# Shorter weight conversion, compact state, keys scaled on ScalarE and a one-instruction leaky rectifier in a retention + two-layer MLP kernel

## The chip, the cores and the metric

One core of a Trainium2 chip runs the whole program. The metric is the device time of one execution in microseconds (us). Beside the times there is one profiled execution of the kernel before, with every instruction's start and duration; all rows of this document come from it.

## The reference, cut to what matters

```python
# attention (retention): B, H, S, D = 4, 8, 768, 64
gamma = 1.0 - 2.0 ** (-5.0 - np.arange(H))
for t in range(S):
    state = gamma * state + einsum('bhd,bhe->bhde', k[:, :, t], v[:, :, t])
    y[:, :, t] = scale * einsum('bhd,bhde->bhe', q[:, :, t], state)
x = y.transpose(0, 2, 1, 3).reshape(3072, 512)
# layer 1 (moe) and layer 2 (moe2): w_in 512 x 2048, w_out 2048 x 512
h = x @ moe_w_in;  x = np.maximum(0.01 * h, h) @ moe_w_out
h = x @ moe2_w_in; x = (h - np.tanh(h)) @ moe2_w_out
```

The weights arrive as 64-bit floating point numbers; the kernel reads them as pairs of 32-bit words and makes 32-bit numbers of them with integer operations.

## The kernel before

**Attention** runs first, in 24 steps over 6 chunks of 128 positions and 4 pairs of heads; a step holds one chunk of one pair for all 4 batches. In step s TensorE transposes the next key tile (L270, `kTp`) and half a query tile (L284, `qTp`), computes the output `y` of step s (L327 inside the chunk, L320 from the carried state `U`), the scores `sc` of step s+1 (L305), and the state's increment `u` (L355). ScalarE copies the transposes out of PSUM (L272 `kT`, L285 `qT`) and the output (L344 `x1st`). VectorE masks the scores (L309, `A`, two instructions a step) and updates the state (L358, two instructions, one for each head's 64 partitions). The state of a pair is kept as 128 x 128 for each batch with two diagonal 64 x 64 blocks and zeros elsewhere, so that one 128-row matmul serves both heads. GpSimd scales the keys of step s+2 (L251) and the queries (L261, four instructions of 128x256 for a query tile). SyncE issues all loads, four steps ahead for keys and values.

**Weight conversion.** A unit is one half (w_in or w_out) of one of 16 weight slices, so 32 units for each layer. `ConvPipe.step()` works on three units at once: `s3` of unit n-2, `s1` of unit n, `s2` of unit n-1. `s1` clamps the high words on VectorE (L103) and squares the result on ScalarE (L106); `s2` is four VectorE instructions (L111, L113, L115, L117); `s3` is `split`, a ScalarE copy into a rounded high part (L126) and a GpSimd subtraction for the low part (L127). A counter sets the pace: the first 13 units are spread over the attention steps from step 6 on, and the rest come at 1.5 units for each MLP step (`RATE` 12 per 8 steps). Each engine runs its instructions strictly in the order of the program, apart from weight loads on TensorE.

**MLP.** 192 steps (2 layers x 6 blocks of 512 rows x 16 slices). A step is 12 matmuls into `h` (L436, three products of high and low parts for each of 4 contraction tiles) and, two steps later, 12 matmuls into four accumulators (L454). Between them stand `el_1` (layer 1: ScalarE copies 0.01 h out of PSUM at L482, VectorE takes the maximum with h at L483) and `el_2` (`split` of the result on ScalarE and GpSimd). Slice m of layer 1 can be used only after units 2m and 2m+1 have gone through `s3`. The units of layer 2 are converted during layer 1, one per two steps, and stored to DRAM until they are reloaded.

Of the kernel before, what the change touches and what calls it, by code (L numbers as in the profile page):

```python
# [18 lines left out]
P = 128  # L19
# [8 lines left out]
F64_MAX_HI = 3.38953138925153547590470800371487866880e38  # L28
# [19 lines left out]
def kernel(  # L48
# [34 lines left out]
    class Convert:  # L83


        def __init__(self, w_in, w_out, m, half, done):
            self.args = (w_in, w_out, m, half)
            self.done = done
            self.id = f"{w_in.tensor.name}_{m}_{half}"
# [9 lines left out]
        def s1(self):  # L99
            pairs = self.raw.rearrange("p (f t) -> p f t", t=2)  # L100
            self.lo, hi = pairs[:, :, 0], pairs[:, :, 1]
            self.y = cm.tile([P, DM], F32, tag="t0", name=f"cy_{self.id}")
            nc.vector.tensor_scalar(out=self.y, in0=hi.bitcast(F32), scalar1=F64_MAX_HI, scalar2=-F64_MAX_HI,  # L103
                                    op0=ALU.min, op1=ALU.max)
            self.sq = cm.tile([P, DM], F32, tag="t1", name=f"csq_{self.id}")
            nc.scalar.activation(out=self.sq, in_=self.y, func=AF.Square)  # L106

        def s2(self):
            y, t = self.y, cm.tile([P, DM], I32, tag="t2", name=f"ct_{self.id}")
            yi = y.bitcast(I32)  # L110
            nc.vector.scalar_tensor_tensor(out=y, in0=self.sq, scalar=F64_MIN_HI_SQ, in1=y,  # L111
                                           op0=ALU.is_ge, op1=ALU.mult)
            nc.vector.tensor_scalar(out=t, in0=yi, scalar1=3, scalar2=0x3FFFFFFF,  # L113
# [26 lines left out]
    for m in range(NM):  # L140
        for half in range(2):
            conv1.append(Convert(moe_w_in, moe_w_out, m, half,
                                 lambda f, m=m, half=half: split(slots[m][:, :, half, :], f, nc.gpsimd)))
            conv2.append(Convert(moe2_w_in, moe2_w_out, m, half,
                                 lambda f, m=m, half=half: nc.sync.dma_start(out=w2s[m, :, half], in_=f)))
# [42 lines left out]
    with tc.tile_pool(name="at", bufs=2, reuse_waits="tile") as at, \  # L188
# [51 lines left out]
        for p in range(NPAIR):  # L240
            u = at.tile([P, NB, P], F32, tag=f"U{p}", name=f"U{p}", bufs=1)
            nc.gpsimd.memset(u, 0.0)
            U.append(u)

        def a_scale_k(s, eng=nc.gpsimd):
# [5 lines left out]
            eng.tensor_tensor(out=t, in0=t, in1=fb, op=ALU.mult)  # L251
# [61 lines left out]
        def a_Y(s):  # L313
# [4 lines left out]
            def inter(first):  # L318
                for b in range(NB):
                    nc.tensor.matmul(y[:, b, :], U[p][:, b, :], d["qT"][:, b, tq], start=first and b == 0,  # L320
                                     stop=b == NB - 1 and not first)
# [25 lines left out]
        def a_U(s):  # L347
            c, p = steps[s]
            d = S[s]
            if c < NC - 1:  # L350
# [5 lines left out]
                for h in range(2):  # L356
                    r = slice(h * ND, (h + 1) * ND)
                    nc.vector.scalar_tensor_tensor(out=U[p][r, :, r], in0=U[p][r, :, r], scalar=gc[r, p:p + 1],  # L358
                                                   in1=u[r, :, :], op0=ALU.mult, op1=ALU.add)
# [116 lines left out]
    def el_1(n):  # L476
# [3 lines left out]
        u = mo.tile([P, TB], F32, tag="u", name=f"u_{n}", bufs=1)  # L480
        if layer == 0:
            nc.scalar.activation(out=u, in_=h, func=AF.Copy, scale=0.01)  # L482
            nc.vector.tensor_tensor(out=gt, in0=u, in1=h, op=ALU.max)  # L483
        else:
            nc.scalar.activation(out=u, in_=h, func=AF.Square)  # L485
# [66 lines left out]

F64_MIN_HI_SQ = 0.0


def _min_sq():
    import numpy as np
    t = float(np.uint32(0x38100000).view(np.float32))
    return t * t


F64_MIN_HI_SQ = _min_sq()


# [51 lines left out]
```

## Time and profile before

| what | value |
|---|---|
| median of 3 runs (lowest to highest) | 1221.44 us (1221.44 to 1222.99) |
| profiled execution: its time, its span | 1223.63 us, 1221.1 us |
| TensorE busy | 1176.3 us, 96% of the span |
| VectorE busy | 759.3 us, 62% |
| ScalarE busy | 518.3 us, 42% |
| GpSimd busy | 425.0 us, 35% |
| mean granted TensorE clock | 0.992 of full speed |

Busy shares are averages over stages that have different limits. The span has three stages: attention until about 140 us, a stretch to about 246 us in which layer 1 has begun while its weights are still being converted, and the rest, in which both layers run on converted weights. The page's row of VectorE in 40 slices rises from 4 to 9 tenths over the first two stages and stays at 7 or below in the third; the row of TensorE has sevens to nines in the first two and nines in the third.

### The profile page before, as it was taken

Reading aid. Unit: us, or ns where it says so; the run is one execution under the profiler, and the core shown is the slowest. Engines: PE = TensorE matmul, PEld = TensorE weight load, DVE = VectorE, ACT = ScalarE, POOL = GpSimd, SP = SyncE. Lnnn points to the kernel's source line nnn. Section 1 sums busy time; section 2 is a strip of 40 time slices with the busy share of each in tenths; the row PEclk is TensorE's granted clock in tenths of the full one; section 3 lists DMA queues with packets and bytes.
Section 4 is the critical chain, followed back from the end, with each engine's and each line's share of the span. In section 5 each row is a group of like instructions: output and inputs, shape, how many; then the busy total and the mean of one; then the engine's idle time right before and its main releaser. Section 6 shows DMA issues by size and latency. Waiting matters only on the chain.

```text
span 1221.1 us, 16090 instructions
## 1 busy us (share of the span) xinstructions
PE 1176.3 (96%) x6059; PEld 967.5 (79%) x6059; DVE 759.3 (62%) x1115; ACT 518.3 (42%) x851; POOL 425.0 (35%) x337
## 2 busy tenths in 40 slices
PE   8978887799999999999999999999999999999998
PEld 6867765578888888888888888888888888888886
DVE  4688899944444544445411477767767677676665
ACT  3343433333333333333344554544544545545543
POOL 4565345433223223223257623223222232232221
PEclk9999998999999999999999999999999999999999
DMA  9997333332142232241062110100100100200000
GB/s 239 269 261 219 117 123 106 103 109 81 69 138 86 78 125 74 78 147 61 18 216 89 54 65 1 47 23 1 69 1 1 69 1 1 70 1 1 35 1 35
DMA packets 108270, 100.22 MB, mean 82 GB/s; under 512 B 54688, under 2 KB 83488, under 8 KB 108192
## 3 DMA queue, kind: packets, MB, share of 16 engines
q1 hardware_dynamic: 105168, 93.87, 24.7%
q10 hardware_dynamic: 3024, 5.32, 1.2%
q8 instruction: 47, 0.77, 0.3%
q14 instruction: 31, 0.25, 0.1%
HBM read 72.96 MB, written 26.21 MB: 81 GB/s over the span
## 4 chain that ended last, share of the span: by engine, by line
PE 83%; DVE 12%; issue 2%; DMA 1%; SPq 1%; ACT 1%; POOL 0%; DVEq 0%; ACTq 0%; POOLq 0%
PE h L436 40%; PE acc L454 39%; DVE _in_moe_w_in_dram L111 3%; DVE _in_moe_w_in_dram L115 2%; DVE _in_moe_w_in_dram L113 2%; DVE _in_moe_w_in_dram L103 1%; DVE A L309 1%; PE sc L305 1%; PE y L327 1%; DVE _in_moe_w_in_dram L117 1%; PE y L320 1%; DVE g L483 1%; PE u L355 1%; DVE U L358 1%; PE kTp L270 0%
## 5 line engine op out<-in xcount | busy, mean ns | idle before, releaser
L436 PE MATMUL h<-xk,w 128*128 128x512 f32 x2304 | 557.8, 391 | 7.2 <-ACT w L126 5.4
L436 PEld LDWEIGHTS h<-xk,w 128*128 128x128 f32 x2304 | 434.5, 189 | 99.8 <-ACT w L126 6.2
L127 POOL TENSOR_TENSOR ghl<-g,ghl 128x512 fp32r<-128x512 f32 x191 | 254.4, 1332 | 616.2 <-ACT ghl L126 616.2
L454 PE MATMUL acc<-ghl,w 128*128 128x512 f32 x1152 | 282.3, 394 | 13.3 <-POOL ghl L127 7.6
L454 PE MATMUL acc<-w,ghl 128*128 128x512 f32 x1152 | 277.2, 389 | 0.5 <-ACT st L467 0.5
L454 PEld LDWEIGHTS acc<-ghl,w 128*128 128x128 f32 x1152 | 218.3, 190 | 62.1 <-POOL ghl L127 9.3
L454 PEld LDWEIGHTS acc<-w,ghl 128*128 128x128 f32 x1152 | 216.0, 188 | 46.6 <-ACT st L467 0.9
L126 ACT ACTIVATE ghl<-g 128x512 fp32r<-128x512 f32 x192 | 120.9, 629 | 296.2 <-DVE g L497 214.2
L483 DVE TENSOR_TENSOR g<-u,h 128x512 f32<-128x512 f32 x96 | 65.8, 686 | 250.7 <-ACT u L482 250.7
L489 DVE SCALAR_TENSOR_TENSOR w<-u,h 128x512 f32<-128x512 f32 x96 | 65.9, 687 | 139.9 <-ACT u L485 139.9
L482 ACT ACTIVATE u<-h 128x512 f32<-128x512 f32 x96 | 57.1, 594 | 142.5 <-PE h L436 140.4
L497 DVE COPY_PREDICATED g<-mk,th 128x512 f32<-128x512 uint8 x96 | 76.7, 799 | 3.3
L117 DVE SCALAR_TENSOR_TENSOR _in_moe_w_in_dram<-_in_moe_w_in_dram,_in_moe_w_in_dram 128x512 int32<-128x512 int32 x60 | 76.2, 1270 | 2.1
L487 ACT ACTIVATE s<-u,lead 128x512 f32<-128x512 f32 x96 | 69.7, 726 | 3.1
L492 DVE SCALAR_TENSOR_TENSOR w<-u,w 128x512 f32<-128x512 f32 x96 | 67.3, 701 | 3.3
L495 DVE SCALAR_TENSOR_TENSOR g<-s,w 128x512 f32<-128x512 f32 x96 | 65.6, 683 | 0.1
L496 DVE TENSOR_TENSOR th<-h,th 128x512 f32<-128x512 f32 x96 | 65.6, 683 | 0.0
L127 POOL TENSOR_TENSOR w<-_in_moe_w_in_dram,w 128x512 fp32r<-128x512 f32 x29 | 39.1, 1347 | 75.7 <-ACT w L126 75.7
L106 ACT ACTIVATE _in_moe_w_in_dram<-_in_moe_w_in_dram 128x512 f32<-128x512 f32 x60 | 37.8, 630 | 63.4 <-DVE _in_moe_w_in_dram L103 63.4
L485 ACT ACTIVATE u<-h 128x512 f32<-128x512 f32 x96 | 56.6, 590 | 14.6 <-PE h L436 14.4
L491 ACT ACTIVATE th<-h 128x512 f32<-128x512 f32 x96 | 57.5, 599 | 4.5 <-DVE w L489 4.4
L111 DVE SCALAR_TENSOR_TENSOR _in_moe_w_in_dram<-_in_moe_w_in_dram,_in_moe_w_in_dram 128x512 f32<-128x512 f32 x60 | 57.2, 953 | 0.0
(59 smaller groups left out, 758.3 us busy)
## 6 DMA issues: line engine op xcount, KB each, us to landing
_in_moe_w_in_dram<-in_moe_w_in_dram SPq DMA_DIRECT2D x29, 512.0 KB, 3.5
_in_moe_w_in_dram<-in_moe_w_out_dram SPq DMA_DIRECT2D x29, 512.0 KB, 3.7
w2s<-_in_moe_w_in_dram SPq DMA_DIRECT2D x32, 256.0 KB, 2.6
w2r<-w2s SPq DMA_DIRECT2D x16, 512.0 KB, 3.3
q<-in_q_dram SPq DMA_DIRECT2D x24, 256.0 KB, 5.0
k<-in_k_dram SPq DMA_DIRECT2D x48, 128.0 KB, 4.0
v<-in_v_dram SPq DMA_DIRECT2D x48, 128.0 KB, 4.1
x2s<-st SPq DMA_DIRECT2D x24, 256.0 KB, 2.0
```

The costliest lines, as they stand in the source:

```text
L111: nc.vector.scalar_tensor_tensor(out=y, in0=self.sq, scalar=F64_MIN_HI_SQ, in1=y, op0=ALU.is_ge, op1=ALU.mult)
L117: nc.vector.scalar_tensor_tensor(out=t, in0=yi, scalar=-0x40000000, in1=t, op0=ALU.bitwise_and, op1=ALU.bitwise_or)
L126: nc.scalar.activation(out=dst[:, 0], in_=src, func=AF.Copy)
L127: eng.tensor_tensor(out=dst[:, 1], in0=src, in1=dst[:, 0].bitcast(F32), op=ALU.subtract)
L436: nc.tensor.matmul(h, a, x[:, b, :], start=kt == 0 and i == 0, stop=kt == NK - 1 and i == 2)
L454: nc.tensor.matmul(ACC[j], a, b, start=m == 0 and i == 0, stop=m == NM - 1 and i == 2)
L483: nc.vector.tensor_tensor(out=gt, in0=u, in1=h, op=ALU.max)
L487: nc.scalar.activation(out=s, in_=u, func=AF.Square, bias=beta)
L489: nc.vector.scalar_tensor_tensor(out=w, in0=u, scalar=C3, in1=h, op0=ALU.mult, op1=ALU.mult)
L492: nc.vector.scalar_tensor_tensor(out=w, in0=u, scalar=A1, in1=w, op0=ALU.add, op1=ALU.mult)
L495: nc.vector.scalar_tensor_tensor(out=gt, in0=s, scalar=K1, in1=w, op0=ALU.add, op1=ALU.mult)
L497: nc.vector.copy_predicated(out=gt, mask=mk, data=th)
```

## The change

Four parts, all visible in the diff:

1. **Conversion.** `s1` becomes one ScalarE instruction (the absolute value of the high words, into tile `t`), and `s2` four VectorE instructions that work in place on `t`: a clamp from below and above, a shift with a mask, and two instructions that merge the low word and the sign and exponent bits from the raw words. The two helper tiles go; `t` rotates over three tags with two buffers each.
2. **Compact state.** `U` is 128 x 64 for each batch instead of 128 x 128 with zeros. One VectorE instruction updates it (the first chunk is a ScalarE copy instead), and the product with the queries becomes two 64 x 64 matmuls for each batch instead of one 128 x 128.
3. **Keys.** From step 2 on the keys are scaled by two ScalarE instructions (one for each head, with the scale in a 128 x 1 operand) instead of one GpSimd instruction.
4. **Leaky rectifier.** In layer 1 one ScalarE instruction (`Prelu`, alpha 0.01) replaces the ScalarE copy and the VectorE maximum.

```diff
         def s1(self):
             pairs = self.raw.rearrange("p (f t) -> p f t", t=2)
-            self.lo, hi = pairs[:, :, 0], pairs[:, :, 1]
-            self.y = cm.tile([P, DM], F32, tag="t0", name=f"cy_{self.id}")
-            nc.vector.tensor_scalar(out=self.y, in0=hi.bitcast(F32), scalar1=F64_MAX_HI, scalar2=-F64_MAX_HI,
-                                    op0=ALU.min, op1=ALU.max)
-            self.sq = cm.tile([P, DM], F32, tag="t1", name=f"csq_{self.id}")
-            nc.scalar.activation(out=self.sq, in_=self.y, func=AF.Square)
+            self.lo, self.hi = pairs[:, :, 0], pairs[:, :, 1]
+            self.t = cm.tile([P, DM], I32, tag=f"t{self.i % 3}", name=f"ct_{self.id}")
+            nc.scalar.activation(out=self.t.bitcast(F32), in_=self.hi.bitcast(F32), func=AF.Abs)
 
         def s2(self):
-            y, t = self.y, cm.tile([P, DM], I32, tag="t2", name=f"ct_{self.id}")
-            yi = y.bitcast(I32)
-            nc.vector.scalar_tensor_tensor(out=y, in0=self.sq, scalar=F64_MIN_HI_SQ, in1=y,
-                                           op0=ALU.is_ge, op1=ALU.mult)
-            nc.vector.tensor_scalar(out=t, in0=yi, scalar1=3, scalar2=0x3FFFFFFF,
+            t, y = self.t, self.t.bitcast(F32)
+            nc.vector.tensor_scalar(out=y, in0=y, scalar1=MIN_HI, scalar2=MAX_HI, op0=ALU.max, op1=ALU.min)
+            nc.vector.tensor_scalar(out=t, in0=t, scalar1=3, scalar2=0x3FFFFFFF,
                                     op0=ALU.logical_shift_left, op1=ALU.bitwise_and)
             nc.vector.scalar_tensor_tensor(out=t, in0=self.lo, scalar=29, in1=t,
                                            op0=ALU.logical_shift_right, op1=ALU.bitwise_or)
-            nc.vector.scalar_tensor_tensor(out=t, in0=yi, scalar=-0x40000000, in1=t,
+            nc.vector.scalar_tensor_tensor(out=t, in0=self.hi, scalar=-0x40000000, in1=t,
                                            op0=ALU.bitwise_and, op1=ALU.bitwise_or)
...
-            u = at.tile([P, NB, P], F32, tag=f"U{p}", name=f"U{p}", bufs=1)
-            nc.gpsimd.memset(u, 0.0)
-            U.append(u)
-
-        def a_scale_k(s, eng=nc.gpsimd):
+            U.append(at.tile([P, NB, ND], F32, tag=f"U{p}", name=f"U{p}", bufs=1))
+
+        def a_scale_k(s, eng=nc.scalar):
...
-            eng.tensor_tensor(out=t, in0=t, in1=fb, op=ALU.mult)
+            if eng is nc.scalar:
+                for h in range(2):
+                    eng.activation(out=t[:, :, h], in_=t[:, :, h], func=AF.Copy, scale=fk[:, 2 * p + h:2 * p + h + 1])
+            else:
+                eng.tensor_tensor(out=t, in0=t, in1=fb, op=ALU.mult)
...
                 for b in range(NB):
-                    nc.tensor.matmul(y[:, b, :], U[p][:, b, :], d["qT"][:, b, tq], start=first and b == 0,
-                                     stop=b == NB - 1 and not first)
+                    for h in range(2):
+                        r = slice(h * ND, (h + 1) * ND)
+                        nc.tensor.matmul(y[r, b, :], U[p][r, b, :], d["qT"][r, b, tq], start=first and b == 0,
+                                         stop=b == NB - 1 and not first)
...
-                for h in range(2):
-                    r = slice(h * ND, (h + 1) * ND)
-                    nc.vector.scalar_tensor_tensor(out=U[p][r, :, r], in0=U[p][r, :, r], scalar=gc[r, p:p + 1],
-                                                   in1=u[r, :, :], op0=ALU.mult, op1=ALU.add)
+                if c == 0:
+                    nc.scalar.activation(out=U[p], in_=u, func=AF.Copy)
+                else:
+                    nc.vector.scalar_tensor_tensor(out=U[p], in0=U[p], scalar=gc[:, p:p + 1], in1=u, op0=ALU.mult,
+                                                   op1=ALU.add)
...
         gt = mo.tile([P, TB], F32, tag="g", name=f"g_{n}", bufs=2)
-        u = mo.tile([P, TB], F32, tag="u", name=f"u_{n}", bufs=1)
         if layer == 0:
-            nc.scalar.activation(out=u, in_=h, func=AF.Copy, scale=0.01)
-            nc.vector.tensor_tensor(out=gt, in0=u, in1=h, op=ALU.max)
+            nc.scalar.activation(out=gt, in_=h, func=AF.Prelu, alpha=0.01)
         else:
+            u = mo.tile([P, TB], F32, tag="u", name=f"u_{n}", bufs=1)
```

How the change moves instructions on two engines. First ScalarE at the start of attention (`kT` are the copies of transposed keys, of steps 0, 1 and 2 in this order; `k` is a key tile being scaled in place). Before:

```order
L285 ACTIVATE qT_152<-qTp_0_153 128x2x2x128
L272 ACTIVATE kT_164<-kTp_159 128x512
L285 ACTIVATE qT_152<-qTp_2_166 128x2x2x128
L272 ACTIVATE kT_198<-kTp_193 128x512
L126 ACTIVATE xk_0_209<-y_200 128x512
L285 ACTIVATE qT_212<-qTp_0_213 128x2x2x128
```

With the change:

```order
L283 ACTIVATE qT_148<-qTp_0_149 128x2x2x128
L270 ACTIVATE kT_160<-kTp_155 128x512
L283 ACTIVATE qT_148<-qTp_2_162 128x2x2x128
L247 ACTIVATE k_128<-k_128,cst 128x4x64 x2
L270 ACTIVATE kT_195<-kTp_190 128x512
L122 ACTIVATE xk_0_206<-y_197 128x512
L283 ACTIVATE qT_209<-qTp_0_210 128x2x2x128
```

The scaling of the keys of step 2, which has to wait for their load, now stands ahead of the copy of the transposed keys of step 1.

Second, VectorE in the stretch in which layer 1 runs and its weights are converted (`cy`, `csq` and `ct` are the conversion's tiles, `g` is the rectifier's result). Before, one MLP step with one unit and the beginning of the next:

```order
L483 TENSOR_TENSOR g_1886<-u_1887,h_1854 128x512
L103 TENSOR_SCALAR cy_in_moe_w_in_dram_0_1894<-raw_in_moe_w_in_dram_0_1839 128x512
L111 SCALAR_TENSOR_TENSOR cy_in_moe_w_in_dram_1_1845<-csq_in_moe_w_in_dram_1_1847,cy_in_moe_w_in_dram_1_1845 128x512
L113 TENSOR_SCALAR ct_in_moe_w_in_dram_1_1898<-cy_in_moe_w_in_dram_1_1845 128x512
L115 SCALAR_TENSOR_TENSOR ct_in_moe_w_in_dram_1_1898<-raw_in_moe_w_in_dram_1_1837,ct_in_moe_w_in_dram_1_1898 128x512
L117 SCALAR_TENSOR_TENSOR ct_in_moe_w_in_dram_1_1898<-cy_in_moe_w_in_dram_1_1845,ct_in_moe_w_in_dram_1_1898 128x512
L103 TENSOR_SCALAR cy_in_moe_w_in_dram_1_1907<-raw_in_moe_w_in_dram_1_1841 128x512
```

With the change:

```order
L109 TENSOR_SCALAR ct_in_moe_w_in_dram_0_1975<-ct_in_moe_w_in_dram_0_1975 128x512
L110 TENSOR_SCALAR ct_in_moe_w_in_dram_0_1975<-ct_in_moe_w_in_dram_0_1975 128x512
L112 SCALAR_TENSOR_TENSOR ct_in_moe_w_in_dram_0_1975<-raw_in_moe_w_in_dram_0_1921,ct_in_moe_w_in_dram_0_1975 128x512
L114 SCALAR_TENSOR_TENSOR ct_in_moe_w_in_dram_0_1975<-raw_in_moe_w_in_dram_0_1921,ct_in_moe_w_in_dram_0_1975 128x512
L109 TENSOR_SCALAR ct_in_moe_w_in_dram_1_2017<-ct_in_moe_w_in_dram_1_2017 128x512
```

A unit is four VectorE instructions instead of five, and the rectifier has none left on VectorE.

## Rows read from the trace of the kernel before

**Rows 1.** The page: its head line, and GB/s moved in 40 slices

```profile
span 1221.1 us, 16090 instructions
...
GB/s 239 269 261 219 117 123 106 103 109 81 69 138 86 78 125 74 78 147 61 18 216 89 54 65 1 47 23 1 69 1 1 69 1 1 70 1 1 35 1 35
```

**Rows 2.** The chain that ended last: start us, us, what

```profile
139.91 5.49 PE h L436 x24
...
253.09 2.72 PE h L436 x12
...
696.45 2.06 PE acc L454 x9
...
703.74 1.65 PE acc L454 x6
...
1205.86 2.73 PE h L436 x12
...
1214.08 3.31 PE acc L454 x12
```

**Rows 3.** VectorE in order of time, attention: start us, us, instruction [idle before]

```profile
46.62 1.29 DVE L309 TENSOR_TENSOR A<-sc,cst 128x512 f32<-128x512 f32 x2 [2.50 <-PE sc L305]
...
65.81 1.29 DVE L309 TENSOR_TENSOR A<-sc,cst 128x512 f32<-128x512 f32 x2
...
70.46 1.29 DVE L309 TENSOR_TENSOR A<-sc,cst 128x512 f32<-128x512 f32 x2 [2.45 <-PE sc L305]
...
101.53 1.29 DVE L309 TENSOR_TENSOR A<-sc,cst 128x512 f32<-128x512 f32 x2
102.73 0.96 DVE L358 SCALAR_TENSOR_TENSOR U<-U,cst,u 64x256 f32<-64x256 f32 x2
103.73 1.07 DVE L103 TENSOR_SCALAR _in_moe_w_in_dram<-_in_moe_w_in_dram 128x512 f32<-128x512 f32 x1
...
108.63 1.29 DVE L309 TENSOR_TENSOR A<-sc,cst 128x512 f32<-128x512 f32 x2
...
136.40 1.28 DVE L309 TENSOR_TENSOR A<-sc,cst 128x512 f32<-128x512 f32 x2
```

**Rows 4.** GpSimd in order of time, the same attention step

```profile
104.47 3.59 POOL L261 TENSOR_TENSOR qp<-q,cst 128x256 f32<-128x256 f32 x4
```

**Rows 5.** VectorE groups of instructions, 46.62 to 136.40 us: xcount, busy us, mean ns, idle before

```profile
L111 DVE SCALAR_TENSOR_TENSOR _in_moe_w_in_dram<-_in_moe_w_in_dram,_in_moe_w_in_dram 128x512 f32<-128x512 f32 x7 | 7.7, 1101 | 0.0
...
L111 DVE SCALAR_TENSOR_TENSOR y_in_moe_w_in_dram<-q_in_moe_w_in_dram,y_in_moe_w_in_dram 128x512 f32<-128x512 f32 x4 | 4.4, 1100 | 0.0
```

**Rows 6.** Busy time, 150 to 243 us: PE, PEld, DVE, ACT, POOL, PE clock, DMA, GB/s

```profile
150.00:243.00 93.00, 74.92 (x292) 57.69 (x290) 89.66 (x103) 35.18 (x62) 46.69 (x33) 0.93 0.36 113
```

**Rows 7.** VectorE groups of instructions, 150 to 243 us

```profile
L483 DVE TENSOR_TENSOR g<-u,h 128x512 f32<-128x512 f32 x12 | 8.2, 679 | 0.0
```

**Rows 8.** VectorE in order of time, three neighbours with no GpSimd instruction beside them

```profile
199.60 0.43 DVE L113 TENSOR_SCALAR _in_moe_w_in_dram<-_in_moe_w_in_dram 128x512 int32<-128x512 int32 x1
200.06 0.69 DVE L115 SCALAR_TENSOR_TENSOR _in_moe_w_in_dram<-_in_moe_w_in_dram,_in_moe_w_in_dram 128x512 int32<-128x512 int32 x1
200.79 0.69 DVE L117 SCALAR_TENSOR_TENSOR _in_moe_w_in_dram<-_in_moe_w_in_dram,_in_moe_w_in_dram 128x512 int32<-128x512 int32 x1
```

**Rows 9.** ScalarE groups of instructions, whole span (L487 has a 128x1 operand)

```profile
L487 ACT ACTIVATE s<-u,lead 128x512 f32<-128x512 f32 x96 | 69.7, 726 | 3.1
...
L126 ACT ACTIVATE w<-_in_moe_w_in_dram 128x512 fp32r<-128x512 f32 x29 | 18.3, 631 | 65.7 <-DVE _in_moe_w_in_dram L117 62.9 <-POOL ghl L127 2.0 <-ACT x1st L344 0.8
```

**Rows 10.** The chain at the start of attention: TensorE's product with the state

```profile
17.86 1.09 PE y L320 x8
```

**Rows 11.** TensorE groups of instructions, 0 to 140 us: the same product

```profile
L320 PE MATMUL y<-qT,U 128*128 128x128 f32 x160 | 22.3, 283 | 0.0
```

**Rows 12.** All engines in order of time, 8 to 18 us

```profile
13.97 1.16 PE L305 MATMUL sc<-qT,kT 64*128 64x128 f32 x16
...
14.65 1.04 POOL L251 TENSOR_TENSOR k<-k,cst 128x512 f32<-128x512 f32 x1
```

More of the change, by code (lines that the diff above doesn't have):

```diff
@@ L26 @@
 TB = NB * P
-F64_MAX_HI = 3.38953138925153547590470800371487866880e38
+MAX_HI = 122879.9921875
+MIN_HI = 2.0 ** -15
 C3 = -0.019799353554844856
@@ L83, with __init__ @@
     class Convert:
-        def __init__(self, w_in, w_out, m, half, done):
-            self.args = (w_in, w_out, m, half)
+        def __init__(self, i, w_in, w_out, m, half, done):
+            self.i, self.args = i, (w_in, w_out, m, half)
             self.done = done
@@ L116, in s2 @@
                                            op0=ALU.logical_shift_right, op1=ALU.bitwise_or)
-            nc.vector.scalar_tensor_tensor(out=t, in0=yi, scalar=-0x40000000, in1=t,
+            nc.vector.scalar_tensor_tensor(out=t, in0=self.hi, scalar=-0x40000000, in1=t,
                                            op0=ALU.bitwise_and, op1=ALU.bitwise_or)
-            self.t = t
         def s3(self):
@@ L141 @@
         for half in range(2):
-            conv1.append(Convert(moe_w_in, moe_w_out, m, half,
+            conv1.append(Convert(len(conv1), moe_w_in, moe_w_out, m, half,
                                  lambda f, m=m, half=half: split(slots[m][:, :, half, :], f, nc.gpsimd)))
-            conv2.append(Convert(moe2_w_in, moe2_w_out, m, half,
+            conv2.append(Convert(len(conv2), moe2_w_in, moe2_w_out, m, half,
                                  lambda f, m=m, half=half: nc.sync.dma_start(out=w2s[m, :, half], in_=f)))
@@ L550 @@
             pipe2.step()
[L553 to L562, printed above, removed]
 def _consts():
```

## The prediction

> **What bounds the kernel now.** I read the chain that ended last first, then VectorE in order of time in each of the first two stages, then the groups of instructions for the prices.
>
> From about 250 us on the chain is nothing but TensorE: groups of 12 matmuls, 2.72 us each [rows 2]. The 192 MLP steps hold 384 such groups, so the MLP cannot take less than 384 x 2.72 = 1044.5 us. It begins at 139.9 [rows 2]; 139.9 + 1044.5 = 1184.4, and the span is 1221.1 [rows 1]. The missing 36.7 us are found in four places [rows 2]. Between the layers TensorE waits from 696.45 + 2.06 = 698.5 to 703.7, 5.2 us. Before the last group it waits from 1208.6 to 1214.1, 5.5 us. The last group takes 3.31 instead of 2.72, and 3.7 us follow it. These 15.0 us lie outside the change. The other 21.7 are lost between 140 and 250 us, while layer 1 runs on weights that are still being converted. So two sums can shrink: the attention stage (139.9) and this loss (21.7).
>
> In the lossy stretch VectorE is the limit: from 150 to 243 us it is busy 89.7 of 93 us, while TensorE has gaps and a granted clock of 0.93 [rows 6]. The stretch holds 12 rectifiers [rows 7], thus 12 MLP steps of 7.75 us where TensorE needs 2 x 2.72 = 5.44. At 1.5 units a step it holds 18 units. Undisturbed, a one-source instruction takes 0.46 us from start to start and a two-source one 0.73 [rows 8]. A unit of two and three is 3.11 us, 18 units 56.0, the rectifiers 8.2 [rows 7]; 28.8 of the 93 us remain. GpSimd ran 33 instructions there [rows 6], so each costs VectorE 28.8 / 33 = 0.87 us.
>
> In attention, the 15 steps from 46.62 to 136.40 take 89.8 us [rows 3]. Eleven of them carry a full conversion, 7 and 4 by the names of their buffers [rows 5], four don't. A step without one takes 4.65 us, and VectorE then sits idle 2.45 us for the scores [rows 3], so TensorE sets that pace. Taking 4.7 for the four, the eleven take (89.8 - 18.8) / 11 = 6.45 each: there VectorE is the limit. The reader can see it from 101.53 to 108.63 [rows 3]: masks, state update, five conversion instructions and the next masks without idle time, while GpSimd scales queries beside them [rows 4]. Its floor is 1.20 + 1.00 + 3.11 = 5.31 [rows 3, 8]; the other 1.14 us of an average step are again waits beside GpSimd.
>
> **The change part by part.**
>
> *Conversion.* Five VectorE instructions become two one-source and two two-source ones, 2 x 0.46 + 2 x 0.73 = 2.38 instead of 3.11 [rows 8]. Two of them work in place, for which there is no row; I take the same price. ScalarE trades one instruction for another of the same size and no longer waits for VectorE before it. The raw buffer is held one instruction longer, 0.7 us, hidden behind loads that are issued three units ahead.
>
> *State.* Two VectorE instructions of 1.00 together [rows 3] become one with as many elements for each partition as one of the two, 0.50. The four cleared tiles at the start were not on the chain. For the first chunk a ScalarE copy replaces the update, off the path. On TensorE, 8 instructions in 1.09 us [rows 10] become 16 on a quarter of the array. The scores also run 16 instructions, on halves of the rows, in 1.16 us [rows 12], so they overlap in pairs. The diagonal quarters have no row. The cost per step lies between nothing, if they overlap as the scores do, and another 1.09, if not. I take nothing, as the scores are the nearest row, and keep the other end as a rival.
>
> *Keys.* GpSimd loses one instruction per step. ScalarE gains two on half a tile each: between 0.32 (half of 0.63) and 0.63, plus 0.1 for the 128x1 operand (0.726 against 0.631) [rows 9], say 0.45 each. ScalarE, busy 42% of the span, has room for that. What counts is the place. At the start, the scaling of step 2 waits for its load ahead of the copy of the transposed keys of step 1, for which the scores at 13.97 wait [rows 12]. GpSimd began this scaling at 14.65 with no wait for the load [rows 12], so the keys landed at 14.65 at the latest. 14.65 + 0.9 + 0.6 for the copy = 16.15, 2.2 us behind 13.97. If they landed 0.7 earlier it is 1.5. I take 1.9. Later steps then run 1.9 behind the loads, and I count no second wait.
>
> *Rectifier.* One ScalarE instruction replaces one, and 0.68 us per step leave VectorE [rows 7]. Against this speaks the Trainium skill, "ScalarE: Activation LUTs", Rules for kernel authors: relu, max and their like belong on VectorE, which is faster for each element. No run here shows Prelu. By that rule the rectifier would stay, the coming stretch would run at 6.64 instead of 5.96 us a step (below), and the sum would be about 4 us higher.
>
> *Sum for attention.* A step with conversion has a VectorE floor of 1.20 + 0.50 + 2.38 = 4.08. What is added for GpSimd lies between nothing (then TensorE's 4.7 rules) and the saturated price, 0.87 for each of 2.7 instructions in an average step (two of the queries, 0.7 subtractions): 6.4. So far 3.7 instructions cost 1.14, or 0.31 each; 2.7 x 0.31 = 0.83 gives 4.9. The loads give another floor: a step moves 1.33 MB (keys, values, queries and output 0.26 each, 0.28 of weights), which at 0.265 MB per us, the rate of the first three slices [rows 1], is 5.0 us. I take 5.1: 11 x 5.1 + 4 x 4.7 = 74.9 instead of 89.8. Attention ends at 139.9 - 14.9 + 1.9 = 126.9.
>
> *Sum for the stretch with conversion.* 18 units x 2.38 = 42.8, plus 33 x 0.87 = 28.7, are 71.5 us for 12 steps, 5.96 a step. Before, 16 steps x (7.75 - 5.44) = 37.0 us of lag cost 21.7, so 15.3 were absorbed by units converted ahead. Now 16 x 0.52 = 8.3 of lag stay below 15.3. I count 1 us for the last units, with ends 0 and 6.
>
> *Total.* 126.9 + 1044.5 + 15.0 + 1.0 = 1187.4 of span, 33.7 less than 1221.1. The profiled execution took 1223.6, and the median of the runs, 1221.44, lies 0.3 above the span; I take the difference from the median: **1188 us**. VectorE's work for layer 2's weights, in layer 1, falls too, but there TensorE hides all of it.
>
> **The rivals.**
>
> *A: VectorE stays the limit beside GpSimd.* For it: denser instructions meet the same subtractions, and in the stretch from 150 us each costs 0.87. Against it: in attention they cost 0.31. At 0.6 a step with conversion is 4.08 + 1.6 = 5.7, 6.6 us more over eleven steps, and the stretch may cost its 6 instead of 1: **1200 us**.
>
> *B: the quarter matmuls don't overlap.* The state's product then takes 2.18. Steps without conversion go to 5.8, those with one from 5.1 to 5.8: 4 x 1.1 + 11 x 0.7 = 12.1, and 4.4 in the four early steps with a state: **1204 us**. For it: both halves write one accumulator tile from different rows of the array, which no row shows; the scores use two tiles. The Trainium skill, "TensorEngine Tiling (Array Packing)", Gotcha 1: PSUM Pressure, says that different row tiles can't access the same PSUM bank at once. By that rule B is the result; no row here shows the case.
>
> *C: slower.* The quarter matmuls run one at a time, each with its whole duration. The mean duration of the instruction is 0.283 us [rows 11]; 16 x 0.283 = 4.5, 3.4 more in each of 20 steps, less 4 hidden: **1252 us**. It decides from 0.19 us for each: (33.7 + 4.4) / 20 = 1.9 more in a step, (1.09 + 1.9) / 16. Against it: no group of TensorE in attention shows instructions apart.
>
> *D: ScalarE meets late keys more than once.* The loads fill the first 90 us, and a key copy behind each late load would cost some 6 us: **1194 us**.
>
> **How the numbers follow.** Forecast 0.64, A 0.16, B 0.12, C 0.04, D 0.04. Low end: all eleven steps at 4.7 (-4.4), keys in time (-1.9), no loss (-1.0) give 1181. High end: A and half of B, 1204. About 0.2% is what a measurement of this kernel can tell from no change; all cases but C are far beyond it. Faster 0.95, same 0.01, slower 0.04.
>
> **What would show it.** Right: the first MLP matmul near 127 us; groups at 2.72 from there with gaps of a few us at most; VectorE at about 0.9 of that stretch or less; about 1.1 us for the state's product with 16 instructions; the second scores near 16 us. Wrong: a product of 2 us or more, conversion steps in attention above 5.5 us with VectorE never idle, or ScalarE idle for key loads after 20 us.

## The result, and the profile after

The changed kernel takes 1186.21 us (median of 4 runs, 1184.64 to 1189.41), the kernel before 1221.49 beside it; the ratio is 0.9712, 95% interval 0.969 to 0.9733. The forecast was 1188 us. The profiled execution is the longest of the four, 1189.41 us, with a span of 1187.6.

The head of the changed kernel's page, its busy times and the data rate in 40 slices:

```profile
span 1187.6 us, 16116 instructions
...
PE 1166.7 (98%) x6219; PEld 961.9 (81%) x6219; DVE 619.4 (52%) x931; ACT 534.7 (45%) x899; POOL 393.3 (33%) x311
...
GB/s 234 248 288 250 159 160 123 97 133 80 93 112 80 120 84 80 150 64 18 158 117 89 71 1 1 72 1 1 71 1 1 72 1 1 72 1 1 36 1 36
```

The third and fourth slice, both in attention, move 288 and 250 GB/s where [rows 1] has 261 and 219: the same loads in less time. The chain that ended last answers to [rows 2]:

```profile
128.67 5.68 PE h L437 x24
...
213.00 3.97 PE h L437 x10
216.97 2.73 PE acc L455 x12
...
670.35 1.66 PE acc L455 x6
672.01 2.74 PE h L437 x12
...
1175.33 8.54 PE acc L455 x36
```

Attention ends at 128.67 (139.91 before), and the last wait of TensorE in the converting stretch ends in the group at 213.00, so from 216.97 on groups follow at 2.72 us. The same point before was 250.35. From there both kernels need the same time to the end: 1187.6 - 216.97 = 970.6 and 1221.1 - 250.35 = 970.8. So the difference of 33.5 us of span lies, but for 0.2, in the two sums of the prediction: 139.91 - 128.67 = 11.2 in attention, and 110.44 - 88.30 = 22.1 in the stretch behind it.

In that stretch TensorE has 29 groups to do, 29 x 2.72 = 78.9 us. It lost 110.4 - 78.9 = 31.5 us before and 88.3 - 78.9 = 9.4 now. All that is neither attention nor this loss comes to 1187.6 - 128.67 - 9.4 = 1049.5 us. For a kernel below, its loss is its span less 1049.5 and less the start of its MLP.

VectorE in order of time in the changed kernel, masks of attention first, then the start of the MLP (start us, us, instruction, [idle before]):

```profile
16.80 0.69 DVE L307 TENSOR_TENSOR A<-sc,cst 128x512 f32<-128x512 f32 x1 [0.95 <-PE sc L303]
...
47.73 1.29 DVE L307 TENSOR_TENSOR A<-sc,cst 128x512 f32<-128x512 f32 x2 [3.33 <-PE sc L303]
...
71.62 1.29 DVE L307 TENSOR_TENSOR A<-sc,cst 128x512 f32<-128x512 f32 x2 [0.33 <-PE sc L303]
...
87.18 1.29 DVE L307 TENSOR_TENSOR A<-sc,cst 128x512 f32<-128x512 f32 x2 [3.10 <-PE sc L303]
...
94.25 1.29 DVE L307 TENSOR_TENSOR A<-sc,cst 128x512 f32<-128x512 f32 x2 [2.19 <-PE sc L303]
...
125.22 1.28 DVE L307 TENSOR_TENSOR A<-sc,cst 128x512 f32<-128x512 f32 x2
...
131.08 0.69 DVE L114 SCALAR_TENSOR_TENSOR _in_moe_w_in_dram<-_in_moe_w_in_dram,_in_moe_w_in_dram 128x512 int32<-128x512 int32 x1
136.06 1.08 DVE L109 TENSOR_SCALAR _in_moe_w_in_dram<-_in_moe_w_in_dram 128x512 f32<-128x512 f32 x1 [4.29 <-ACT _in_moe_w_in_dram L105]
...
140.93 0.42 DVE L109 TENSOR_SCALAR _in_moe_w_in_dram<-_in_moe_w_in_dram 128x512 f32<-128x512 f32 x1
...
152.81 0.42 DVE L109 TENSOR_SCALAR _in_moe_w_in_dram<-_in_moe_w_in_dram 128x512 f32<-128x512 f32 x1
```

The fifteen steps that took 89.8 us in [rows 3] take 125.22 - 47.73 = 77.5. The first five of them run at 4.78 us, TensorE's own pace. Then come steps like 87.18 to 94.25, 7.1 us, with VectorE idle: there something else is late. At the start of the MLP VectorE stands idle 4.29 us for ScalarE. From 140.93 to 152.81 it makes three units in 11.88 us, that is two MLP steps of 5.94 us.

Two more readings. The product with the state is in the chain with sixteen instructions in hardly less than the 1.09 us of [rows 10]:

```profile
20.00 1.02 PE y L320 x16
```

And the chain of the second half of attention goes through transfers:

```profile
84.67 6.48 DMA k<-in_k_dram
...
100.69 4.97 DMA q<-in_q_dram
105.73 5.85 DMA x1s<-x1st
112.86 4.82 DMA _in_moe_w_in_dram<-in_moe_w_in_dram
```

### The profile page after: what moved, and what is told of

Its sections match the earlier page's. It is cut to its first block, busy times and chain, and to the rows that moved or that the text cites. A ratio compares the mean times of both kernels' runs of the same rounds, so it can differ in the third digit from the quotient of the medians.

```text
span 1187.6 us, 16116 instructions
## 1 busy us (share of the span) xinstructions
PE 1166.7 (98%) x6219; PEld 961.9 (81%) x6219; DVE 619.4 (52%) x931; ACT 534.7 (45%) x899; POOL 393.3 (33%) x311
## 4 chain that ended last, share of the span: by engine, by line
PE 87%; DVE 5%; DMA 3%; issue 2%; SPq 1%; ACT 1%; POOL 0%; ACTq 0%
PE h L437 41%; PE acc L455 41%; DVE _in_moe_w_in_dram L112 3%; PE sc L303 2%; DMA k<-in_k_dram 1%; SPq L202 1%; PE y L327 1%; DVE _in_moe_w_in_dram L109 1%; DVE _in_moe_w_in_dram L110 1%; PE y L320 1%; PE u L355 1%; PE kTp L268 1%; DMA x1s<-x1st 0%; PE qTp L282 0%; DMA q<-in_q_dram 0%
## 5 line engine op out<-in xcount | busy, mean ns | idle before, releaser
L455 PE MATMUL acc<-ghl,w 128*128 128x512 f32 x1152 | 277.3, 389 | 2.3 <-POOL ghl L123 2.3
L109 DVE TENSOR_SCALAR _in_moe_w_in_dram<-_in_moe_w_in_dram 128x512 f32<-128x512 f32 x61 | 30.8, 506 | 218.2 <-ACT _in_moe_w_in_dram L105 218.2
L482 ACT ACTIVATE g<-h 128x512 f32<-128x512 f32 x96 | 57.2, 596 | 144.0 <-PE h L437 144.0
L123 DVE TENSOR_TENSOR xk<-xr,xk 128x512 fp32r<-128x512 f32 x22 | 23.6, 1110 | 137.6 <-ACT xk L122 137.6
L487 ACT ACTIVATE s<-u,lead 128x512 f32<-128x512 f32 x96 | 69.7, 726 | 3.1
L112 DVE SCALAR_TENSOR_TENSOR _in_moe_w_in_dram<-_in_moe_w_in_dram,_in_moe_w_in_dram 128x512 int32<-128x512 int32 x58 | 64.3, 1109 | 2.0
L485 ACT ACTIVATE u<-h 128x512 f32<-128x512 f32 x96 | 56.6, 589 | 13.6 <-PE h L437 13.3
L114 DVE SCALAR_TENSOR_TENSOR _in_moe_w_in_dram<-_in_moe_w_in_dram,_in_moe_w_in_dram 128x512 int32<-128x512 int32 x58 | 57.8, 997 | 2.0
L123 POOL TENSOR_TENSOR w<-_in_moe_w_in_dram,w 128x512 fp32r<-128x512 f32 x29 | 38.7, 1336 | 50.4 <-ACT w L122 50.3
```

What stands on the lines that cost most here:

```text
L112: nc.vector.scalar_tensor_tensor(out=t, in0=self.lo, scalar=29, in1=t, op0=ALU.logical_shift_right, op1=ALU.bitwise_or)
L114: nc.vector.scalar_tensor_tensor(out=t, in0=self.hi, scalar=-0x40000000, in1=t, op0=ALU.bitwise_and, op1=ALU.bitwise_or)
L123: eng.tensor_tensor(out=dst[:, 1], in0=src, in1=dst[:, 0].bitcast(F32), op=ALU.subtract)
L455: nc.tensor.matmul(ACC[j], a, b, start=m == 0 and i == 0, stop=m == NM - 1 and i == 2)
L487: nc.scalar.activation(out=s, in_=u, func=AF.Square, bias=beta)
```

## The experiments

Each is an edit of the changed kernel. Measured times are medians of 4 runs; times of stages are from the one profiled execution of each.

### The four parts, undone one at a time

```diff
 # u_rect
-nc.scalar.activation(out=gt, in_=h, func=AF.Prelu, alpha=0.01)
+nc.scalar.activation(out=u, in_=h, func=AF.Copy, scale=0.01)
+nc.vector.tensor_tensor(out=gt, in0=u, in1=h, op=ALU.max)
 # u_keys
-def a_scale_k(s, eng=nc.scalar):
+def a_scale_k(s, eng=nc.gpsimd):
 # u_state
-U.append(at.tile([P, NB, ND], F32, tag=f"U{p}", name=f"U{p}", bufs=1))
+u = at.tile([P, NB, P], F32, tag=f"U{p}", name=f"U{p}", bufs=1)
+nc.gpsimd.memset(u, 0.0)
...
 # u_conv
-nc.scalar.activation(out=self.t.bitcast(F32), in_=self.hi.bitcast(F32), func=AF.Abs)
+nc.vector.tensor_scalar(out=self.y, in0=hi.bitcast(F32), scalar1=F64_MAX_HI, scalar2=-F64_MAX_HI,
+                        op0=ALU.min, op1=ALU.max)
+nc.scalar.activation(out=self.sq, in_=self.y, func=AF.Square)
...
```

**u_rect**, the rectifier in two instructions again. 

> The changed kernel with the rectifier put back on two engines (ScalarE copy of 0.01 h, VectorE maximum). Theory (VectorE is still the limit in the stretch where layer 1 runs and its weights are converted, 5.94 us a step against TensorE's 5.44): 0.68 us more on VectorE in each of 16 steps, so the stretch grows from 88.3 us by about 11 and the time goes from 1186 to about 1197; attention stays at 128.7. Rival (the rectifier is hidden, the gain came from the conversion alone): the time stays within 2 us of 1186.

Measured: 1195.42 us (1194.66 to 1199.76), 9.2 more. Its MLP begins at 126.95 and the loss is 1194.3 - 126.95 - 1049.5 = 17.9 instead of 9.4, 8.5 more where about 11 was expected. The theory holds. By the rule in the Trainium skill, "ScalarE: Activation LUTs", Rules for kernel authors, VectorE would be the place for it; the reason given there is a rate in bf16, and these operands are f32. Here VectorE isn't the place: what counts is which engine is the limit, and ScalarE pays the same for either instruction (row L482 below: 596 ns; the scaled copy in u_rect took 597).

**u_state**, the 128x128 state with two updates. 

> The changed kernel with the 128 x 128 state, its two updates on VectorE and the full matmul put back. Theory (attention is now paced by TensorE and the loads, VectorE has room): attention ends 1 to 3 us later than 128.7, mostly the product's 1.09 instead of 1.02 us in 20 steps; time 1187 to 1190. Rival (VectorE is still the limit of the steps with a conversion): 0.5 us in each of eleven steps, attention at 134 or later, time 1192 or more.

Measured: 1185.43 us (1184.69 to 1191.3), ratio to before 0.9712, as for the change itself. The state part brings nothing that can be measured; the rival falls. The theory's 1 to 3 us more didn't come either: the MLP begins at 126.67.

**u_keys**, the keys scaled on GpSimd again. 

> The changed kernel with the keys scaled on GpSimd again. Theory (on ScalarE the scaling of the keys stands ahead of the copies that TensorE waits for, and late key loads hold it up): the second scores start near 14.0 instead of 14.7 us, at full clock, and no key load stands in the chain of attention; attention ends 2 to 4 us earlier, at about 125 to 127, time 1183 to 1185. Rival (GpSimd's 22 scalings cost VectorE 0.31 to 0.87 us each, and that is why they were moved): attention ends 4 us or more later than 128.7, time 1190 or more.

Measured: 1188.5 us (1188.13 to 1188.81), between the two, and not clear of the change, whose four runs reach from 1184.64 to 1189.41. The early wait is gone (second masks at 14.73 instead of 16.80), and still the MLP begins at 128.02. Its chain from 80 to 128 us runs through VectorE's conversion and masks, with instructions stretched beside GpSimd (1.40 us where 0.43 is the short duration):

```profile
87.88 0.68 DVE A L307
88.55 0.39 DVE U L359
88.94 0.35 DVE _in_moe_w_in_dram L109
89.31 1.40 DVE _in_moe_w_in_dram L110
```

So the move of the keys takes a cost from VectorE and puts a wait for loads on ScalarE; what is left of the two at the end can't be told from nothing.

**u_conv**, the old conversion. 

> The changed kernel with the old conversion put back (clamp on VectorE, square on ScalarE, then four VectorE instructions). Theory: one more two-source VectorE instruction of 0.73 us for each unit. In the stretch with layer 1 that is 1.1 us a step over 16 steps, about 17 us; in attention the steps with a conversion become VectorE's again, 3 to 6 us; time about 1186 + 22 = 1208 (1203 to 1212). Rival (the waits beside GpSimd, not the number of VectorE instructions, set the pace of the stretch): less than 10 us more, time below 1196.

Measured: 1205.52 us (1202.55 to 1208.59), 19.3 more. The MLP begins 4.4 us later (133.08), the loss is 1204.3 - 133.08 - 1049.5 = 21.7, 12.3 more where about 17 was expected. The theory holds: this part carries more than half of the gain, and most of it behind attention.

### What is left of the loss: the late start

```diff
 # f_early: the loop of pipe1.step() is moved ahead of el_1(n1), and counts n1 + 1
-            while pipe1.n < ATT_UNITS + RATE * n1 // 8:
+            while pipe1.n < ATT_UNITS + RATE * (n1 + 1) // 8:
```

> Edit: while layer 1 starts, the conversion calls of a step stand ahead of that step's rectifier instead of behind it. Theory: the changed kernel loses 4.3 us at the start of layer 1 because the conversion's first instruction, now on ScalarE, stands there behind a rectifier that waits for TensorE, while VectorE is idle; since VectorE sets the pace of the whole stretch, those 4.3 us come off the end: 1182 us (1181 to 1184), with no VectorE idle time above 2 us between 131 and 137. Rival 1: the raw weights land too late there in any case (issue to landing 4.2 us), so the idle time stays and the time is within 1 us of 1186. Rival 2: the idle time goes, but VectorE's lag at the end of the stretch is set by the units and not by their start: also within 1 us of 1186.

Measured: 1185.45 us (1184.2 to 1186.03), no difference from 1186.21. The idle time is gone: VectorE goes from 129.75 to 135.59 without a gap, at the place of the 4.29 us. But the loss only falls to 1184.2 - 127.27 - 1049.5 = 7.4, because TensorE meets another wait, for GpSimd, which no expectation had (the change has it too, but shorter: 1.35 us before 182.14). TensorE in order of time in f_early:

```profile
187.46 0.49 PE L455 MATMUL acc<-ghl,w 128*128 128x512 f32 x1 [0.41 <-ACT ghl L122]
190.10 4.19 PE L455 MATMUL acc<-ghl,w 128*128 128x512 f32 x11 [2.15 <-POOL ghl L123]
```

The low part of a step's result came late because GpSimd made a low part of the next input right before it (from 186.97 us); the eleven matmuls behind that wait take 4.19 us, where eleven took 2.79 at 181.54. A wait at the front of a saturated stretch was not worth its length.

### GpSimd beside VectorE

```diff
 # f_wsub: in the stretch, low parts of the weights
-eng.tensor_tensor(out=dst[:, 1], in0=src, in1=dst[:, 0].bitcast(F32), op=ALU.subtract)   # GpSimd
+nc.vector.tensor_tensor(out=dst[:, 1], in0=src, in1=dst[:, 0].bitcast(F32), op=ALU.subtract)
 # f_allsub: and low parts of the results of the first 16 steps
-split(g, Q.pop(n), nc.gpsimd if n < NT - 1 else nc.vector)
+split(g, Q.pop(n), nc.gpsimd if NM <= n < NT - 1 else nc.vector)
 # g_dummy: f_allsub, and in each of the first 16 steps
+for _ in range(2):
+    nc.gpsimd.tensor_tensor(out=dm, in0=dm, in1=dm, op=ALU.subtract)
```

**f_wsub.** 

> Edit: in the stretch where layer 1 runs on weights being converted, the subtractions that form the low parts of the weights run on VectorE instead of GpSimd (24 instructions; the results' low parts stay on GpSimd). Theory: each GpSimd subtraction beside VectorE costs VectorE about 0.87 us there, more than the 0.73 us that the same subtraction costs VectorE itself, so moving 1.5 of them a step changes the pace from 5.94 to about 5.75 us a step and the time to 1184 us (1182 to 1187). Rival: VectorE's long instructions there have another cause than GpSimd (loads, ScalarE's writes); then 1.5 x 0.73 = 1.1 us a step come on top, some 15 us over the stretch: 1200 us (1196 to 1204).

Measured: 1179.23 us (1176.95 to 1181.26), 7.0 less than the change.

**f_allsub.** 

> Edit: as f_wsub, and the low parts of layer 1's results are also formed on VectorE for the first 16 steps, so that GpSimd hardly runs in the stretch. Theory: 2.5 subtractions a step at 0.73 instead of 0.87 us: about 5.6 us a step, 1184 us (1181 to 1187), and every VectorE instruction in the stretch at its short duration (0.43 and 0.69 us). Rival: GpSimd's share is not what stretches them: 2.5 x 0.73 = 1.8 us a step on top, some 25 us: 1211 us (1205 to 1216).

Measured: 1176.99 us (1174.76 to 1181.31), ratio to before 0.9635, 95% interval 0.9602 to 0.9668: faster than both kernels. The loss is 1179.5 - 129.01 - 1049.5 = 1.0 us in f_wsub and 1173.0 - 122.96 - 1049.5 = 0.5 in f_allsub. Both gained more than the theory said: f_wsub's window below holds 18 units, thus 12 steps of 5.42 us, which is TensorE's own pace and not the 5.75 of the theory.

Busy times from 140 to 205 us (PE, PEld, DVE, ACT, POOL, each with its instructions, PE clock, DMA share, GB/s), for the change:

```profile
140.00:205.00 65.00, 61.47 (x267) 49.65 (x267) 63.31 (x66) 31.40 (x56) 41.48 (x29) 1.00 0.46 144
```

for f_wsub:

```profile
140.00:205.00 65.00, 65.00 (x288) 53.83 (x287) 63.15 (x90) 34.81 (x61) 20.81 (x14) 1.00 0.51 162
```

and for f_allsub:

```profile
140.00:205.00 65.00, 65.00 (x289) 53.83 (x288) 56.82 (x97) 34.00 (x61) 2.66 (x2) 1.00 0.47 145
```

In the same 65 us VectorE does 97 instructions instead of 66 and is less busy; TensorE has no gap left. What the stretching is can be seen in the groups of VectorE's instructions in that window, in the change:

```profile
L112 DVE SCALAR_TENSOR_TENSOR _in_moe_w_in_dram<-_in_moe_w_in_dram,_in_moe_w_in_dram 128x512 int32<-128x512 int32 x17 | 29.6, 1743 | 0.6
L114 DVE SCALAR_TENSOR_TENSOR _in_moe_w_in_dram<-_in_moe_w_in_dram,_in_moe_w_in_dram 128x512 int32<-128x512 int32 x17 | 22.4, 1319 | 0.6
L110 DVE TENSOR_SCALAR _in_moe_w_in_dram<-_in_moe_w_in_dram 128x512 int32<-128x512 int32 x16 | 7.8, 489 | 0.5
L109 DVE TENSOR_SCALAR _in_moe_w_in_dram<-_in_moe_w_in_dram 128x512 f32<-128x512 f32 x16 | 7.7, 483 | 0.0
```

and in f_allsub:

```profile
L114 DVE SCALAR_TENSOR_TENSOR _in_moe_w_in_dram<-_in_moe_w_in_dram,_in_moe_w_in_dram 128x512 int32<-128x512 int32 x17 | 13.9, 815 | 0.6
...
L112 DVE SCALAR_TENSOR_TENSOR _in_moe_w_in_dram<-_in_moe_w_in_dram,_in_moe_w_in_dram 128x512 int32<-128x512 int32 x16 | 11.1, 693 | 0.6
```

The short durations are 0.42, 0.43, 0.69 and 0.69. In the change the four groups take 67.5 us where these would give 16 x 0.85 + 34 x 0.69 = 37.1; the other 30.4 fall on 29 GpSimd instructions, 1.05 us each. For f_wsub the same working gives 14.0 us on 14, 1.0 each. (Busy times of one group overlap the next by some 0.1 us, so the sums are larger than the window.) One such pair, GpSimd and VectorE in order of time in the change:

```profile
138.40 1.34 POOL L123 TENSOR_TENSOR w<-_in_moe_w_in_dram,w 128x512 fp32r<-128x512 f32 x1
```

```profile
138.62 1.67 DVE L112 SCALAR_TENSOR_TENSOR _in_moe_w_in_dram<-_in_moe_w_in_dram,_in_moe_w_in_dram 128x512 int32<-128x512 int32 x1
140.32 0.69 DVE L114 SCALAR_TENSOR_TENSOR _in_moe_w_in_dram<-_in_moe_w_in_dram,_in_moe_w_in_dram 128x512 int32<-128x512 int32 x1
```

The VectorE instruction starts 0.22 us behind GpSimd's and takes 0.98 too long, while GpSimd's has 1.12 to go; the next one, alone, takes 0.69. The Trainium skill, "SBUF — State Buffer", section "SBUF: two separate sides", says that GpSimd and a VectorE instruction with two inputs from SBUF share a pair of ports under an exclusive lock, so that the one that comes second waits for the other's whole instruction. These rows agree with it to 0.14 us: the stretched instruction ends 0.55 us behind GpSimd's, at 140.29, where 0.69 would be its whole duration.

**g_dummy** shuts out that f_wsub and f_allsub gained by ending TensorE's waits for GpSimd rather than by freeing VectorE. 

> Edit: f_allsub, and GpSimd makes two 128x512 subtractions a step in layer 1's first 16 steps, on a tile that nobody reads or waits for. Theory: a GpSimd subtraction stretches the VectorE instructions beside it by about 1.0 us, wherever its result goes; VectorE then needs 1.5 x 2.86 + 0.6 + 2 x 1.0 = 6.9 us a step and the stretch loses some 16 us: 1193 us (1188 to 1197). Rival: what f_wsub and f_allsub took away was TensorE's wait for low parts that came late from GpSimd, not the stretching; then nobody notices the added work: within 2 us of f_allsub (1175 to 1179).

Measured: 1194.39 us (1193.19 to 1195.24), 17.4 more than f_allsub, by work that nobody waits for. The loss is 1192.7 - 124.94 - 1049.5 = 18.3. TensorE's waits are now for VectorE (TensorE in order of time):

```profile
149.21 4.72 PE L464 MATMUL acc<-ghl,w 128*128 128x512 f32 x11 [3.51 <-DVE ghl L128]
...
196.29 3.41 PE L446 MATMUL h<-xk,w 128*128 128x512 f32 x10 [3.46 <-DVE w L175]
```

The rival falls: GpSimd's price for VectorE is shown as a cause.

### What bounds attention now

```diff
 # f_novload: in a_load, later steps use the sixth step's values
-load_kv(s, "v", v)
+if s < 6:
+    load_kv(s, "v", v)
+else:
+    S.setdefault(s, {})["v"] = v5[0]
 # g_order: f_allsub, and the third step's keys are scaled behind a_Tk(1)
 # g_att10: f_allsub, with
-ATT_UNITS = 13
+ATT_UNITS = 10
-RATE = 12
+RATE = 14
```

**f_novload.** 

> Edit: attention loads values for its first six steps only; all later steps use the sixth step's values again (18 loads of 0.26 MB less). Theory: the slower half of the changed attention (5.1 to 7.1 us a step instead of 4.8 from 72 us on) waits for loads; without these its steps go back to about 4.8 us, so that attention ends some 4 to 6 us earlier, at 122 to 124 us, and the time is 1181 to 1183 us. Rival: the wait is VectorE beside GpSimd or TensorE itself; attention then ends within 1.5 us of 127.5 and the time is within 1.5 us of 1186.

Measured: 1182.39 us (1181.48 to 1184.65). The MLP begins at 120.55, even earlier than expected. Busy times of its second half of attention:

```profile
70.20:120.50 50.30, 49.25 (x717) 41.40 (x717) 42.30 (x65) 33.76 (x65) 25.73 (x25) 1.00 0.77 221
```

and of the same steps in the change:

```profile
71.60:128.67 57.07, 50.83 (x717) 42.61 (x717) 44.03 (x65) 33.31 (x65) 23.33 (x25) 0.97 0.90 255
```

The instructions are the same, but with fewer loads they take 50.3 instead of 57.1 us; TensorE is then busy 49.25 of 50.3. The theory holds: the second half of attention waits for loads. The loss behind it is 9.6, as in the change, so what attention saved came off the end. Between these two profiles that is 8 us, but the change's is its longest run and this one the shortest of its four; between the medians it is 3.8.

**g_order.** 

> Edit: f_allsub, and the scaling of the third step's keys stands on ScalarE behind the copy of the second step's transposed keys instead of ahead of it. Theory: the early wait of the changed kernel (second masks at 16.8 instead of 15.2 us) goes, but attention waits for loads later on and takes it back, as in u_keys: second masks at about 15 us, the first matmul of layer 1 within 123 to 128.5 us, time within 1.5 us of f_allsub (1175.5 to 1178.5). Rival: the 1.6 us come off the end: 1175 us or less, the first matmul of layer 1 at 121.4 us or less.

Measured: 1177.27 us (1175.19 to 1179.23), the same as f_allsub; second masks at 15.26, the MLP from 123.68. The time is the theory's, but it doesn't show that the early wait is worth nothing: in f_allsub's profile little of it was left to win. There the second masks stand at 15.47 and the third at 20.24, against 19.83 in g_order and 22.15 in the change.

**g_att10.** 

> Edit: f_allsub, with 10 instead of 13 weight units converted during attention, and 1.75 instead of 1.5 units a step behind it. Theory: attention is limited by loads; three units are 1.57 MB of raw weights, at the 0.264 MB per us that ran there 6 us, and the pace without load waits is 4.75 us a step: the first matmul of layer 1 comes at 119 to 122 us. VectorE without GpSimd beside it takes 1.75 x 2.86 + 0.6 = 5.6 us a step, 0.16 over TensorE's 5.44, so the stretch loses 0 to 3 us: 1171 us (1169 to 1175). Rival: attention is limited by something else, or the late units make TensorE wait as long: 1177 us or more.

Measured: 1178.44 us (1177.07 to 1182.78); no gain. The MLP began at 121.16, within the expected 119 to 122 and 1.8 ahead of f_allsub's profile, but the loss is 1175.3 - 121.16 - 1049.5 = 4.6, more than the 0 to 3 expected, and with it the rival's time came out. TensorE waits for the units that now come last, four times in a row of this kind (TensorE in order of time):

```profile
188.70 2.60 PE L446 MATMUL h<-xk,w 128*128 128x512 f32 x10 [0.58 <-DVE w L175]
195.01 2.58 PE L446 MATMUL h<-xk,w 128*128 128x512 f32 x10 [0.54 <-DVE w L175]
201.93 2.57 PE L446 MATMUL h<-xk,w 128*128 128x512 f32 x10 [1.17 <-DVE w L175]
```

**g_att10o**, both together. 

> Edit: g_att10 and g_order together. Theory: with fewer loads behind it, the early wait is no longer taken back by later load waits, so that its 1.6 us now count: 1.0 to 2.0 us less than g_att10. Rival: no difference beyond 0.7 us from g_att10.

Measured: 1179.09 us (1176.14 to 1179.38), 0.65 above g_att10, where 1 to 2 less was expected. The time is the rival's. But here too little was left to win: the third masks came at 20.13 against 20.44 in g_att10. What the early wait is worth stays open. f_allsub, 9.2 us under the change, has the lowest median; the runs of f_wsub, g_order, g_att10 and g_att10o overlap with its own.

## Why the prediction held

The sum named 126.9 + 1044.5 + 15.0 + 1.0 = 1187.4 of span; the profiled span is 1187.6. The agreement is better than the steps are: attention took 1.8 us more than its term, what lies outside the two sums 10.0 less, and the stretch lost 8.4 more. That these cancel to 0.2 is luck. The high end of the range is also added up wrong: A and half of B give 1188 + 12 + 8 = 1208, not 1204.

- **Attention, 126.9.** 128.67 here, between 126.67 and 128.02 in u_rect, u_state and u_keys. A conversion step was taken at 5.1 us, and the fifteen steps at 74.9; they took 77.5. Of the two ends given, the TensorE pace of 4.7 is what VectorE's work allows (4.78 up to 71.6 us), and the floor by loads, 5.0 us a step, is what holds the rest. That floor was in the working, but as one of two about equal reasons; f_novload shows it to be the one that decides. Its rate was misread: 0.265 MB per us is the mean of the second and third slice of [rows 1]; the first three give 0.256, which makes the floor 5.2, and 77.5 us over fifteen steps are 5.17 each. Rival D, key copies waiting for late loads, came true in part: ScalarE's scaling waited 13.2 us, 11.4 of them for keys, 4.4 in the early wait and 7.0 after 20 us, which the prediction had named as a sign of being wrong (the groups of ScalarE over the span):

```profile
L247 ACT ACTIVATE k<-k,cst 128x256 f32<-128x256 f32 x44 | 20.2, 500 | 13.2 <-DMA k<-in_k_dram 11.4 <-ACT x1st L344 0.9 <-DMA q<-in_q_dram 0.9
```

- **The early wait, 1.9.** The second masks came at 16.80 instead of 15.16 before, 1.6 later. The mechanism was right, the size by luck: the second scores began at 14.69, only 0.7 behind the 13.97 of before and not near 16, because the keys landed by 13.25, when their scaling began. The other 0.9 is the duration of these scores, 2.08 us at a granted clock of 0.50 instead of 1.16, which the working didn't have. That the wait counts in full at the end is not shown, nor that it counts for nothing: u_rect and f_early have their third masks at 22.51 and 22.46, later than the change's 22.15, and begin the MLP earlier, at 126.95 and 127.27.

- **The stretch.** The pace on VectorE was predicted as 5.96 us a step and is 5.94, with two errors that cancel: the 5.96 has 33 / 12 = 2.75 GpSimd instructions a step at 0.87 us, the two for the next input included, and the 5.94 has 2.5 at (11.88 - 3 x 2.38) / 5 = 0.95. The step that failed is the account around it, *15.0 us outside* and *15.3 absorbed*. The gaps of 5.2 us between the layers and 5.5 us before the last group were read from the chain, but the chain there only leaves TensorE for other engines, and TensorE works on. TensorE in order of time, before:

```profile
699.01 2.88 PE L436 MATMUL h<-xk,w 128*128 128x512 f32 x12
701.73 1.52 PE L454 MATMUL acc<-w,ghl 128*128 128x512 f32 x6
703.74 1.65 PE L454 MATMUL acc<-w,ghl 128*128 128x512 f32 x6 [0.49 <-ACT st L467]
...
1208.42 8.95 PE L454 MATMUL acc<-w,ghl 128*128 128x512 f32 x36
```

 Only 0.49 us is idle. So the stretch had lost 31.5 us, not 21.7, and of the 37.0 of lag 5.5 were absorbed, not 15.3. With that the same pace gives 16 x 0.50 - 5.5 = 2.5 us of loss, not nothing. The change's 9.4 are this, about 2.0 for two low parts of the next input that GpSimd makes beside VectorE (there three units, 176.59 to 190.44, took 13.85 instead of 11.88), and the 4.3 of the late start, together 8.8; but f_early shows that such pieces don't simply add up, since without the late start 7.4 remain. Two errors of the sum met: too much was put outside (15.0 where 5.0 remain), too little inside (1.0 where 9.4 are).

- **A move that was costed at nothing.** The conversion's first instruction went to ScalarE, "of the same size", and indeed takes 657 ns. But on ScalarE it stands behind the rectifier, which waits for TensorE; this is the 4.29 us of idle VectorE. The text had named only the wait that was removed on ScalarE, not the queue that the step joined.

```profile
L482 ACT ACTIVATE g<-h 128x512 f32<-128x512 f32 x96 | 57.2, 596 | 144.0 <-PE h L437 144.0
...
L105 ACT ACTIVATE _in_moe_w_in_dram<-_in_moe_w_in_dram 128x512 f32<-128x512 f32 x58 | 38.1, 657 | 1.2 <-DMA _in_moe_w_in_dram<-in_moe_w_in_dram 1.2
```

- **The rectifier.** Priced right a step (0.68), too low in the end (4 us by the sum without it, 9.2 measured), through the same 15.3.

- **The state.** The product takes 1.02 us for sixteen instructions, so the nearest row, the scores, was the right one to take; B and C fall. The rule of "TensorEngine Tiling (Array Packing)", Gotcha 1, in the Trainium skill, by which B would have been the result, is not borne out here: two row halves wrote one accumulator tile in the time of the eight larger instructions. What VectorE saves on the update is real but hidden, and was never split off in the sum.

- **A.** VectorE beside GpSimd did stay the limit of the stretch (63.3 of 65 us busy, 0.97 and not the 0.9 named as a sign of being right), as the sum itself had it, at nearly the price taken: 0.95 us start to start, where 0.87 was taken. In attention A fell: its conversion steps ran at 4.78 until loads were late.

## What to carry to other kernels

A gap in the chain of waits is idle time of an engine only if that engine's own order of time shows it idle; look there before a gap is booked as fixed. Price an instruction of GpSimd by what it does to VectorE's neighbours: in a stretch where VectorE is the limit, a 128x512 subtraction on GpSimd cost VectorE 1.0 us, and 0.69 when VectorE did it itself. And when a step moves to another engine, write down what stands ahead of it in that queue.

## What was not expected of the hardware

- The attention stage, once it waits for loads, ends at different times from the same instructions. The change, u_rect, f_early, f_wsub, f_allsub and g_dummy have the same attention; the MLP began between 122.96 us (f_allsub) and 129.01 (f_wsub), and f_allsub's four runs range over 6.6 us. So a profiled span can stand some us off its median (f_allsub's profiled run is its shortest), and a difference of 1 or 2 us between two versions is not shown by these runs. Why loads come later in one execution than in another was not tried.
- After a wait of 1.06 us in the second step the scores ran at 2.08 us instead of 1.16 [rows 12]. The granted clock in this stretch of the change was 0.50, the lower of the two levels (1.2 GHz). In f_allsub they ran at 1.16 after a wait of 1.08 us, with a granted clock of 1.00 from 13.70 to 18.70 (TensorE in order of time in the change and in f_allsub, then the busy times of the change):

```profile
14.69 2.08 PE L303 MATMUL sc<-qT,kT 64*128 64x128 f32 x16 [1.06 <-ACT kT L270]
```

```profile
14.28 1.16 PE L312 MATMUL sc<-qT,kT 64*128 64x128 f32 x16 [1.08 <-ACT kT L279]
```

```profile
14.70:16.70 2.00, 2.00 (x16) 1.78 (x16) 0.69 (x1) 0.95 (x2) 0.00 (x0) 0.50 1.06 295
```

 The group at 213.00, behind two waits, took 3.97 us; the granted clock from 213.00 to 216.97 was 0.62. So such a wait can cost more than its length, and doesn't in every execution.
